# V's overlapping rows loaded once and copied on the chip, with a new issue order, in a one-core attention, mixture and MLP kernel

## The chip, the core and the metric

One core of a Trainium2 chip runs the whole program. The metric is the device time of one execution in microseconds, lower is better. The engines are TensorE (PE, with its weight loads PEld), VectorE (DVE), ScalarE (ACT), GpSimd (POOL) and SyncE (SP), which here only issues DMAs. Each engine works through its own instructions in the order in which the program issued them; semaphores tie the engines together.

## The reference

Three blocks in a row, all in float32, on B=2, H=8, S=768, D=64:

```
k_sum = k.reshape(B,H,24,32,D).max(3);  v_sum = v.reshape(B,H,24,32,D).mean(3)
scores_l = scale * q @ k.T,  kept where |i-j| < 16, else -1e9
scores_s = scale * q @ k_sum.T + log(32)
a = softmax(concat([scores_l, scores_s]));   x = a @ concat([v, v_sum])
# x as [B, S, 512] into 4 causal attention experts with top-2 gates,
# summed, then u = x + low-rank mix along S, out = u + relu(u @ w_ch1) @ w_ch2
```

The change touches the first block (the windowed attention) and one store at the very end.

## The kernel before, in words

**Stages.** The 16 heads form 8 pairs p = 0..7. A pair has 12 query blocks of 64 rows; a slot s covers four of these blocks for both heads, so a pair has 3 slots and the first block 24 slots. A query block of 64 rows sees a window of 96 keys (64 plus 15 or 16 on each side), so neighbouring windows overlap by 32 rows. After the first block come the projections and the causal attention of the experts (`v_proj`, `qk_proj`, `s_row`, `t_bank`, `pv`), then the merged MLP for batch 0 (`w1c`, `mlp1`, `mlp2`) and for batch 1 (`mlp1x`, `mlp2x`, `wide_sum`, `wide_store`).

**One pair of the first block.** `load_k`, `load_q` and `load_v` issue DMAs on SP. `load_v` (L377) brings V as the host has laid it out: for each head a tile of 96 partitions by 12 blocks by 65 numbers, block m holding rows 64m to 64m+95, so the 32 overlapping rows come twice from memory. There are three V buffers (`VWT`, one per p mod 3); the load of pair p+3 waits until the last `a_pv` of pair p has read the buffer. `kmax` (DVE) takes the maximum of K over 32 rows. `kcopy` (L404) spreads K into a window layout with the factor -1/8: per head columns 0 to 63, then columns 64 to 95, then the 24 block maxima; POOL does it for pairs 1 to 7, and for pair 0 it is split over POOL, ACT (`act.mul`, L412) and DVE. `fill_k` and `fill_q` write masks and identities into the other half of the partitions, once per buffer. `vsum` (L380) sums V over 32 rows on PE with a picking matrix, ACT and DVE add the four partial sums, and `vcast` (POOL) spreads them into the V tile.

**One slot.** `a_scores` (16 PE instructions in the trace, L431, then one DVE minimum, L434, and four ACT exponentials, L437), `a_trans` (4 transposes, L442, and one ACT copy, L444), `a_pv` (16 instructions, L454, then a reciprocal and a product on DVE) and `a_out` (2 transposes, L468, one ACT cast, L473, one DVE subtraction, L249).

**The order.** Every function is registered with `at(...)`; a function that yields is cut into parts. The table `TIMES` gives each part its place in one global order (0 to 1925), and `BANKS` gives each part its PSUM bank. That global order is what every engine's queue is made of; nothing is reordered later. The first PE work is `wake_up`: 24 products of a zeroed tile, to have PE busy from the start. `wake_zero` (L337) zeroes that tile on DVE.

**The end.** `wide_store` (L969) adds two parts of the last 256 rows' results and issues the stores on SP; the last row block is stored in two halves.

Of the kernel before, what the change touches and what calls it, by code (L numbers as in the profile page):

```python
# [22 lines left out]
NP = H // 2  # L23
QT = 64
# [7 lines left out]
KPAD = S + QT  # L32
# [3 lines left out]
def f(ap):  # L36
# [164 lines left out]
def tile_block_attention_moe_mixer(ctx: ExitStack, tc: tile.TileContext, qT, kP, vW, vB, wm, woT, wo,  # L201
# [134 lines left out]

    def wake_zero():  # L337
        dve.memset(wake, 0.0)

    def wake_up(n):  # L340
        for _ in range(n):
            pe.matmul(bank(7)[:, 0:128], wake, wake, start=True, stop=True)
# [34 lines left out]
    def load_v(p, h):  # L377
        nc.sync.dma_start(VWT[p % NBUF][0:WCOL, h], vW[p, :, h])
# [899 lines left out]
```

## Time and profile before

| | us |
|---|---|
| median of 3 runs | 426.53 |
| the three runs | 426.52, 426.53, 429.07 |
| the profiled execution, its own time | 428.55 |
| span of the profiled execution, first to last instruction | 426.7 |
| PE busy in it | 416.8 (98%) |
| DVE, ACT, POOL busy | 294.1, 242.7, 203.6 |
| moved by DMA | 35.01 MB |

The profiled execution took 428.55 us, of which 426.7 us lie between its first and its last instruction and 1.85 us around them. The granted TensorE clock was 1.000 over the span, which is the level of 2.4 GHz. A line of the trace names its engine, the kernel's line, what is written and read, the shape and the count; the time in brackets is what the engine stood idle before it, and for what. PE's ends are modelled, so the starts are the better guide to its pace.

### The profile page before, as it was taken

What the parts mean: (1) busy time and instruction counts of PE and PEld (TensorE: products, weight loads), DVE (VectorE), ACT (ScalarE), POOL (GpSimd) and SP (SyncE); (2) the same over time, 40 slices, a digit from 0 to 9 for tenths busy, and PEclk for the clock granted to TensorE, in tenths of its full rate; (3) what the DMA queues carried; (4) which work ended last, traced back from release to release, by engine and by line L of the source; (5) the groups of instructions that cost most, each with busy time, mean ns of one, the idle gap of its engine ahead of it and who ended that gap; (6) DMA issues with size and microseconds to landing.
All of it is one profiled execution on the core that took longest, in us unless ns stands there. A gap on an engine that the chain in (4) does not pass through costs nothing.

```text
span 426.7 us, 9493 instructions
## 1 busy us (share of the span) xinstructions
PE 416.8 (98%) x3568; PEld 384.0 (90%) x3568; DVE 294.1 (69%) x784; ACT 242.7 (57%) x615; POOL 203.6 (48%) x287
## 2 busy tenths in 40 slices
PE   7999999999999999999998999999999999999995
PEld 6898999999979898978897989989889999999995
DVE  6788745887658677877845885374577886755664
ACT  4589766566856696985555544452454355344341
POOL 6998765538886888643152642333543332000000
PEclk9999999999999999999999999999999999999999
DMA  8887670000212015312234452311103000100001
GB/s 218 222 218 210 200 168 2 3 0 20 68 51 78 0 51 174 100 50 95 89 109 153 147 167 86 124 69 51 49 27 123 2 2 1 51 2 0 26 26 49
DMA packets 14499, 35.01 MB, mean 82 GB/s; under 512 B 1907, under 2 KB 3187, under 8 KB 14454
## 3 DMA queue, kind: packets, MB, share of 16 engines
q1 hardware_dynamic: 14454, 34.41, 26.5%
q8 instruction: 28, 0.46, 0.4%
q14 instruction: 17, 0.14, 0.1%
HBM read 31.26 MB, written 3.15 MB: 81 GB/s over the span
## 4 chain that ended last, share of the span: by engine, by line
PE 44%; issue 4%; POOL 1%; DMA 1%; DVE 1%; DVEq 0%; POOLq 0%
PE ps L953 13%; PE ps L994 12%; PE ps L921 8%; PE ps L981 6%; PE ps L544 3%; PE ps L1003 2%; DMA x<-in_w_dram 1%; POOL x L276 1%; POOL m L276 1%; DVE a L971 0%; POOL m L910 0%; DVE a L988 0%; DVE a L963 0%; DVE a L962 0%; DVE a L965 0%
## 5 line engine op out<-in xcount | busy, mean ns | idle before, releaser
L246 POOL TENSOR_SCALAR a<-a 64x384 fp32r<-64x384 f32 x64 | 33.7, 527 | 12.8 <-ACT a L670 7.6
L981 PE MATMUL ps<-x,w1h 128*128 128x384 f32 x128 | 37.7, 341 | 1.6 <-DVE a L988 1.1
L921 PE MATMUL ps<-x,w1h 128*128 128x256 f32 x192 | 37.6, 282 | 0.0
L665 PE MATMUL ps<-x,m 128*128 128x384 f32 x192 | 36.4, 340 | 0.0
L665 PEld LDWEIGHTS ps<-x,m 128*128 128x128 f32 x192 | 33.2, 188 | 0.3 <-issue 0.2
L720 POOL TENSOR_SCALAR ex<-ex,rs,gate 128x512 f32<-128x512 f32 (+5 forms) x36 | 25.5, 716 | 12.1 <-ACT ex L707 5.6
L921 PEld LDWEIGHTS ps<-x,w1h 128*128 128x128 f32 x192 | 31.0, 189 | 0.2
L988 DVE SCALAR_TENSOR_TENSOR a<-ps,a 128x384 fp32r<-128x384 f32 x32 | 17.6, 552 | 18.9 <-ACT a L986 18.9
L986 ACT ACTIVATE a<-ps 128x384 fp32r<-128x384 f32 x32 | 15.6, 490 | 25.4 <-PE ps L981 23.1
L249 DVE TENSOR_TENSOR x<-x,x 128x384 fp32r<-128x384 f32 (+1 forms) x28 | 18.7, 677 | 14.5 <-ACT x L928 8.2
L696 PE MATMUL ps<-a 128*128 128x384 f32 (+4 forms) x128 | 27.8, 337 | 0.3 <-DVE lg L625 0.3
L921 PE MATMUL ps<-x,w1l 128*128 128x256 f32 x96 | 27.0, 282 | 0.0
L981 PEld LDWEIGHTS ps<-x,w1h 128*128 128x128 f32 x128 | 23.6, 188 | 3.6 <-DVE a L988 1.6
L704 DVE CUSTOM_DVE_ANT_0 ex<-ps,cc 128x384 f32<-128x384 f32 (+5 forms) x36 | 20.8, 598 | 8.6 <-PE ps L696 3.5
L994 PE MATMUL ps<-m,a 128*128 128x512 f32 x108 | 26.3, 392 | 0.0
L707 ACT ACTIVATE ex<-ex,nmx 128x256 f32<-128x256 f32 (+5 forms) x36 | 23.4, 651 | 3.7 <-DVE nmx L704 2.5
L267 DVE SCALAR_TENSOR_TENSOR x<-x 128x256 uint32<-128x256 uint32 (+3 forms) x38 | 23.6, 631 | 1.7 <-ACT x L265 1.7
L263 DVE TENSOR_SCALAR x<-x 128x256 uint32<-128x256 uint32 (+3 forms) x38 | 18.0, 479 | 9.2 <-DMA x<-in_w_dram 8.5
L994 PEld LDWEIGHTS ps<-m,a 128*128 128x128 f32 x108 | 20.1, 188 | 3.9
L737 ACT COPY pt<-ps 128x384 f32<-128x384 f32 (+1 forms) x40 | 19.9, 523 | 6.1 <-PE ps L729 4.3
L249 DVE TENSOR_TENSOR a<-a,a 128x384 fp32r<-128x384 f32 (+1 forms) x24 | 14.8, 622 | 10.4 <-ACT a L928 7.9
L265 ACT ACTIVATE x<-x 128x256 f32<-128x256 f32 (+3 forms) x38 | 20.7, 553 | 2.1 <-DMA x<-in_w_dram 2.0
(330 smaller groups left out, 1230.5 us busy)
## 6 DMA issues: line engine op xcount, KB each, us to landing
x<-in_w_dram SPq DMA_DIRECT2D x16, 512.0 KB, 3.6
x<-in_w_dram SPq DMA_DIRECT2D x20, 256.0 KB, 2.7
vb<-in_vW_dram SPq DMA_DIRECT2D x5, 585.0 KB, 5.7
a<-in_kP_dram SPq DMA_DIRECT2D x7, 416.0 KB, 6.2
out_dram<-a SPq DMA_DIRECT2D x11, 256.0 KB, 2.1
x<-in_wm_dram SPq DMA_DIRECT2D x4, 386.0 KB, 6.3
tb<-in_w_dram SPq DMA_DIRECT2D x6, 256.0 KB, 3.8
a<-in_w_dram SPq DMA_DIRECT2D x6, 256.0 KB, 2.9
```

What stands on the lines that cost most here:

```text
L246: pool.tensor_scalar(dst, src, 1.0, 0.0, op0=ALU.mult, op1=ALU.add)
L249: dve.tensor_tensor(dst, src, f(hi), op=ALU.subtract)
L267: dve.scalar_tensor_tensor(low, high, 3, low, op0=ALU.logical_shift_left, op1=ALU.bitwise_or)
L665: pe.matmul(acc, (WML if wl else WMH)[k][:, 128 * e:128 * e + 128], xt(b, k, xl)[:, c], start=n == 0, stop=n == 11)
L696: pe.matmul(flat[:, base + c0:base + c1], QS[u][:, 128 * i:128 * i + 128], kk[:, c0:c1], start=x == 0, stop=x == 1)
L704: dve.tensor_tensor_reduce(out=ex[:, 0:W], in0=flat[:, base:base + W], in1=cmask[:, S - W:S], scale=-1.0 / 8.0, scalar=3.0e38, op0=ALU.add ...
L707: act.activation(ex[:, 0:W], ex[:, 0:W], AF.Exp, bias=nmx, scale=-1.0, accum_out=sums)
L720: pool.tensor_scalar(ex, ex, rs[:, i % 2:i % 2 + 1], gate[b][:, i, e:e + 1], op0=ALU.mult, op1=ALU.mult)
L921: pe.matmul(acc[:, 256 * i:256 * i + 256], (W1L if wl else W1H)[q][:, c, 128 * (ff % 2):128 * (ff % 2) + 128], cp(1, c, xl)[:, o], start=m ...
L953: pe.matmul(acc[:, 256 * hf:256 * hf + 256], v[:, BLK[a]], w[wl], start=g < 2 and q == 0 and hf == 0 and i == 0, stop=q == 7 and i == 2, s ...
L981: pe.matmul(acc, (W1L if wl else W1H)[ff // 2][:, c, 128 * (ff % 2):128 * (ff % 2) + 128], cp(b, c, xl)[:, o], start=n == 0, stop=n == 5)
L994: pe.matmul(out_bank(b, 3 * j + t), a[:, 128 * t:128 * t + 128], w, start=False, stop=ff == 15 and x == 2, skip_group_check=True)
```

## The change

- **V.** For pair 0 the load stays. For pairs 1 to 7 `load_v` issues two DMAs: partitions 32 to 95 of both heads and all blocks, and partitions 0 to 31 of block 0 alone. The other 11 blocks' first 32 rows are copied on the chip by a new function `vdup`, one DVE copy for head 0 and one ACT copy for head 1, from partitions 64 to 95 of the block before.
- **K.** `kcopy` writes the 96 window columns with one instruction in place of two; K's padded length goes from 832 to 800 (`KPAD` to `KEND`).
- **Start.** `wake_zero` issues, behind the zeroing, a multiplication of one column on ACT, ahead of all other ACT work.
- **End.** The first half of the last row block's store is issued on ACT's queue in place of SP's.
- **Order.** `TIMES` and `BANKS` are replaced as a whole (761 functions with 1913 places in place of 774 with 1926).

```diff
-KPAD = S + QT
+KEND = S + WCOL - QT
 ...
     def wake_zero():
         dve.memset(wake, 0.0)
+        first = sm.tile([128, 1], F32, name="first", tag="first", bufs=1)
+        act.mul(first, wake[:, 0:1], 1.0)
 ...
     def load_v(p, h):
-        nc.sync.dma_start(VWT[p % NBUF][0:WCOL, h], vW[p, :, h])
+        vw = VWT[p % NBUF]
+        if p == 0:
+            nc.sync.dma_start(vw[0:WCOL, h], vW[p, :, h])
+        else:
+            nc.sync.dma_start(vw[32:WCOL], vW[p, 32:])
+            nc.sync.dma_start(vw[0:32, :, 0], vW[p, 0:32, :, 0])
+
+    def vdup(p):
+        vw = VWT[p % NBUF]
+        dve.tensor_copy(vw[0:32, 0, 1:], vw[64:WCOL, 0, 0:NQ - 1])
+        act.copy(vw[0:32, 1, 1:], vw[64:WCOL, 1, 0:NQ - 1])
 ...
         if o < WCOL:
-            src = KPT[p % 2][r, o:o + S].rearrange("p (m n) -> p m n", n=QT)[:, mm, 0:n]
+            t = KPT[p % 2][r, QT * mm.start:]
+            src = bass.AP(t.tensor, t.offset, [t.ap[0], [QT, mm.stop - mm.start], [1, n]])
 ...
-        nc.sync.dma_start(out[1, 128 * t:128 * t + 128, c], sb[:, c])
+        (nc.scalar if s == 2 and i and not c.start else nc.sync).dma_start(out[1, 128 * t:128 * t + 128, c], sb[:, c])
 ...
-                for o, n in ((0, QT), (QT, WCOL - QT), (WCOL, NB)):
+                for o, n in ((0, WCOL), (WCOL, NB)):
                     at(t + 0.001, kcopy, p, hh, mm, o, n)
+        if p:
+            at(A(PER * p) + Z["vs"] - 0.1, vdup, p)
```

Read off the old and the new `TIMES`, the order at the start is this (SP: DMAs; the number is the pair for loads, `vsum`, `vdup` and the slot for `a_...`):

| queue | before | after |
|---|---|---|
| SP | K0 (2), V0 (2), pick, K1, V1, Q0 (4), Q1 (2), eps, K2, Q2, eps, V2 | K0 (2), Q0 (3), pick, V1 (2), Q0, K1, V0, eps, V0, Q1, eps, Q1, K2, V2 (2), Q2 |
| PE | 18 wake-ups, vsum 0, 6 wake-ups, vsum 1, a_scores 0, 1, 2, a_trans 0, a_scores 3, 4, a_trans 1, 2, a_scores 5, a_pv 0, 1, 2, vsum 2 | 21 wake-ups, vsum 1, a_scores 0, 1, 2, vsum 0, a_trans 0, 1, 2 wake-ups, a_trans 2, 1 wake-up, a_scores 3, 4, 5, a_pv 0, 1, 2, vsum 2 |
| ACT | kcopy 0 in 4 pieces, fill_k, kcopy 0 in 4 pieces among two vsum copies, exponentials of slots 0, 1, 2, a_trans copies | the one-column product, kcopy 0 in 2 pieces, fill_k, vdup 1, kcopy 0 in 2 pieces, exponentials 0, 1, vsum 0, exponentials 2, vsum 1, a_trans copies, vdup 2, exponentials 3, 4 |
| DVE, ahead of a_scores 0 | masks, kmax 0, fill_k, vsum 0, kmax 1 | wake_zero, masks, fill_k, kmax 0, vdup 1, kmax 1 |

Later in the first block, `vsum` 6 moves from behind the first five `v_proj` parts to ahead of them. Between `a_pv` 11, which frees its V buffer, and `vsum` 6 PE then has eleven parts: `a_out` 8 to 11, `a_trans` 12 to 14, `a_scores` 15 and 16, `a_pv` 12 and 13.

## Rows read from the trace of the kernel before

**Rows 1.** The page's part 1: busy time, share and count by engine

```profile
PE 416.8 (98%) x3568; PEld 384.0 (90%) x3568; DVE 294.1 (69%) x784; ACT 242.7 (57%) x615; POOL 203.6 (48%) x287
```

**Rows 2.** Windows: length, PE, PEld, DVE, ACT, POOL busy, clock, DMA share, GB/s

```profile
2.00:12.50 10.50, 9.03 (x76) 8.36 (x76) 7.96 (x32) 5.30 (x11) 8.09 (x16) 1.00 1.01 259
...
22.50:51.00 28.50, 28.42 (x553) 26.06 (x552) 23.27 (x61) 24.75 (x74) 23.85 (x32) 1.00 0.79 217
```

**Rows 3.** Timeline of PE, first 25 us: start, length, line, count, idle before

```profile
2.32 6.44 PE L342 MATMUL ps<-vst 128*128 128x128 f32 x36 [2.32 <-DVE vst L338]
...
12.47 0.86 PE L385 MATMUL ps<-vb,cc 96*32 96x128 f32 x24 [0.35 <-DMA vb<-in_vW_dram]
13.27 0.43 PE L431 MATMUL ps<-pt,ex 128*64 128x120 f32 x4
...
14.14 0.39 PE L431 MATMUL ps<-pt,ex 128*64 128x120 f32 x4
...
20.89 1.10 PE L454 MATMUL ps<-vb,w1h 121*64 121x65 f32 x32
...
23.68 0.60 PE L442 MATMUL ps<-cc,tb 128*121 128x128 f32 x4
24.11 0.60 PE L442 MATMUL ps<-cc,ex 128*121 128x128 f32 x4
```

**Rows 4.** DMA issues of the page: count, KB each, median us to landing

```profile
vb<-in_vW_dram SPq DMA_DIRECT2D x5, 585.0 KB, 5.7
...
a<-in_kP_dram SPq DMA_DIRECT2D x1, 272.0 KB, 2.5
...
cc<-in_vB_dram SPq DMA_DIRECT2D x1, 27.0 KB, 4.5
```

**Rows 5.** Timeline of SP, first 14 us: start of the issue

```profile
2.58 0.43 SPq L353 DMA_DIRECT2D cc<-in_vB_dram  x1
...
13.23 0.29 SPq L347 DMA_DIRECT2D vb<-in_cst_dram  x1
```

**Rows 6.** Timeline of all engines, 1 to 15 us: what ACT, POOL, DVE do

```profile
1.27 0.20 DVE L327 TENSOR_SCALAR a<-a 64x96 f32<-64x96 f32 x1
...
2.10 0.17 DVE L338 MEMSET vst<- 128x128 f32 x1
...
3.79 1.28 ACT L412 ACT_TABLE_LOAD   x1 [3.79 <-DMA a<-in_kP_dram]
...
5.60 0.24 POOL L419 TENSOR_SCALAR pt<-a 64x64 f32<-64x64 f32 x1
...
6.85 0.40 DVE L365 COPY c<-a 64x480 f32<-64x480 f32 x1
6.86 0.50 POOL L419 TENSOR_SCALAR pt<-a 64x64 f32<-64x64 f32 x1
...
7.01 0.98 ACT L363 COPY c<-a 64x960 f32<-64x960 f32 x1
...
11.57 0.95 DVE L402 TENSOR_REDUCE ks<-a 128x24 f32<-128x768 f32 x1
...
13.07 0.82 POOL L419 TENSOR_SCALAR w1h<-a 64x768 f32<-64x768 f32 x1
...
14.45 0.51 POOL L419 TENSOR_SCALAR w1l<-a 64x384 f32<-64x384 f32 x1
```

**Rows 7.** Timeline of ACT: two sets of exponentials one behind the other

```profile
16.69 1.12 ACT L437 ACTIVATE ex<-ps,nmx 128x120 f32<-128x120 f32 x4
17.66 1.15 ACT L437 ACTIVATE pt<-ps,nmx 128x120 f32<-128x120 f32 x4
```

**Rows 8.** Waits of PE over the span: total us, times, longest

```profile
PE ps L981 <- DVE a L988: 1.1, 1, 1.1
```

**Rows 9.** Timeline of the end: the last sums on DVE, the last stores

```profile
422.14 1.35 DVE L971 TENSOR_TENSOR a<-ps,a 128x512 f32<-128x512 f32 x3
422.90 1.30 SPq L974 DMA_DIRECT2D out_dram<-a  x3
```

More of the change, by code (lines that the diff above doesn't have):

```diff
@@ L280, in tile_block_attention_moe_mixer @@
                                               ("pt0", S), ("tb", 512), ("w1h0", 2048), ("w1l0", 2048), ("w1l1", 2048),
-                                              ("w1h1", 2048), ("a1", 2 * KPAD), ("a0", 3 * S), ("woh", 1024), ("wol", 1024))}
+                                              ("w1h1", 2048), ("a1", 2 * KEND), ("a0", 3 * S), ("woh", 1024), ("wol", 1024))}
     KC, NK, NBUF = NQ * KCOL, 3, 3
-    KPT = [regs["a1"][:, o:o + KPAD] for o in (0, KPAD)]
+    KPT = [regs["a1"][:, o:o + KEND] for o in (0, KEND)]
     KWT = [[regs[n][:, 0:KC].rearrange("p (m n) -> p m n", m=NQ) for n in nn] for nn in (("pt1", "c32"), ("w1h0", "w1l0"))]
@@ L1040, in tile_block_attention_moe_mixer @@
         at(-29, wake_up, n)
-    KP, QP, VP, MP = (FIRST, KPAD), (256, S), (1, 2), (2, 4, NQ)
+    KP, QP, VP, MP = (FIRST, KEND), (256, S), (1, 2), (2, 4, NQ)
     at(-20, distances)
@@ L1211, in _layout @@
     pad = WIN - 1
-    kp = np.zeros((B * NP, 128, KPAD), k.dtype)
+    kp = np.zeros((B * NP, 128, KEND), k.dtype)
     kp[:, :, pad:pad + S] = k.transpose(0, 1, 3, 2).reshape(B * NP, 128, S)
```

284 rows, old and new, of tables (BANKS, TIMES) are left out of this document.

## The prediction

> **What bounds the kernel.** I read the totals by engine first, then the windows of the first block, PE's timeline of the start, the DMA issues with SP's timeline, and the end. The totals say that PE is the bound: 416.8 us busy of a span of 426.7 [rows 1]. The change removes no product, so it can only gain from PE's idle time: some 10 us, plus the wake-up products that stand at the start because nothing else is ready. In 22.5 to 51 us PE is busy 28.42 of 28.50 us; there the reader should look at the neighbours, ACT with 24.75, POOL with 23.85 and DVE with 23.27 us of 28.5 [rows 2]. They are hidden, but with little room.
>
> The room is at the two ends. At the start PE does wake-ups from 2.32 us; `vsum` 1 waits at 12.47 for V of pair 1, a_scores 0 follows at 13.27, and a_pv 0, from where PE has work without a break, starts at 20.89 [rows 3]. In 2 to 12.5 us the DMA engines are full, share 1.01 at 259 GB/s [rows 2]: the start is a question of which bytes come first. Then SP issues nothing more until 13.23, where it waits for DVE [rows 5]. At the end the last sums run from 422.14 and the three last stores are issued one behind the other from 422.90 for 1.30 us, 0.43 each [rows 9].
>
> **The start, step by step.** K0, V0 and the small pick tile, 1028 KB, had landed 4.5 us behind the pick's issue at 2.58, so at 7.1 [rows 4, 5]. In the new order V1 ends the first 1089 KB (K0 400, Q0 256, pick 27, V1 406). 61 KB more at 259 GB/s are 0.2 us: V1 lands at 7.3 in place of 12.47. `vdup` 1 on ACT moves 715 numbers per partition; between nothing and the 960 of L363 at 0.98 us [rows 6] I take 0.78 as an estimate by size. It ends at 8.1.
>
> PE's wake-ups: 36 instructions took 6.44 us [rows 3], 0.177 each. 42 now stand ahead of `vsum` 1. `wake_zero` takes the place where the masks began, 1.27 in place of 2.10 [rows 6], so PE starts near 1.5 and ends them at 8.9. So the wake-ups, not V1, release `vsum` 1: 8.9, and with its 0.80 (12.47 to 13.27) a_scores 0 comes at 9.7. What else does a_scores 0 need? Behind `vdup` 1 ACT has two kcopy pieces, by L363's pace 0.8 and 0.4: done at 9.3. In time. The table load of 1.28 us, which began only when K had landed at 3.79 [rows 6], now lies ahead of that landing; if it did not, 9.3 would be 10.6 and the start 0.9 later.
>
> Three a_scores at 0.87 (13.27 to 14.14) end at 12.3. `vsum` 0 needs V0, which now ends the first 2208 KB (1089, Q0 128, K1 400, V0 585, eps 6): 1180 KB behind the mark at 7.1, 4.7 us at full rate, so 11.8; but by the same sum V1 would have come at 11.0 before and came at 12.47, so up to 13.2. I take 12.5, and 13.3 behind `vsum`. Then three a_trans at 0.43 (23.68 to 24.11), three wake-up products of two instructions (1.1), three a_scores (2.6), and 0.1 to 0.2 for a change of kind here and there: a_pv 0 at 18.4 in place of 20.89, **-2.5 us**. Bounds: -2.9 with V0 at once, -2.1 with V0 at 13.2. POOL's merged K copies and K1 come inside this: K1 at some 10 us, then a DVE maximum of 0.95 [rows 6] ahead of the minimum of slot 0, 11.6 for a product that a_trans 0 uses at 13.3.
>
> **The first block.** Seven `vdup` add 7 x 0.78 = 5.5 us to ACT. On DVE 715 numbers cost more than the 0.40 of 480 [rows 6]; at most in proportion, 0.60: some 0.55, 3.9 us in all. In 22.5 to 51 us about four fall: 3.1 us on ACT against 3.75 idle, 2.2 us on DVE against 5.2 idle [rows 2]. ACT's busy time counts ends twice: two sets of exponentials of 1.12 and 1.15 us start 0.97 apart [rows 7], so its room is larger than it looks. I take them as hidden under PE; uncovered they cost up to 5.5. POOL saves: 768 and 384 columns cost 0.82 and 0.51 [rows 6], one of 1152 by the slope between them 1.15, 0.18 less; 14 of them give 2.5 us, hidden, so nothing. The memory traffic falls by 7 x 179 KB, some 5 us of a DMA that is not the bound behind 22.5 us (share 0.79): nothing. The small second DMA of 64 rows of 260 bytes: a tile with rows of 216 bytes came in among the full queues at the usual 4.5 us [rows 4], so nothing; the issue on SP, 0.43 more per pair, lies inside each load's time.
>
> The Trainium skill speaks against the DVE copy: "SBUF — State Buffer", section "SBUF: two separate sides", says that a DVE operation in a two-port mode and a GpSimd operation exclude each other for the whole instruction. The trace agrees: a POOL copy of 64x64 took 0.24 us alone and 0.50 beside the DVE copy of 0.40 [rows 6]. By that rule seven DVE copies push POOL back by 3.9 us at most, against the 2.5 saved.
>
> The one tight wait that I find is `vsum` 6. Between a_pv 11 and it PE has 4 a_out (half an a_trans each, 0.9), 3 a_trans (1.3), 2 a_scores (1.7) and 2 a_pv (32 instructions 1.10, so 1.0): 4.9 us. In that time V6 must be issued (0.43), land and be copied (0.78). For 390 KB the landing lies between 2.5 (272 KB) and 5.7 (585 KB) [rows 4]; by size 3.7. That makes 4.9, late by nothing, from -1.2 to +2.0. While ACT and DVE stand at this copy, exponentials and minima queue behind it, so I take **+0.3**. Pairs 3 and 4 have some 6.7 us by the same counting.
>
> **The middle and the end.** Behind the first block the products are the same in a new order. PE's longest wait there was 1.1 us, for DVE's L988 [rows 8]. Such waits may go or come: 0, bounds -1.5 and +2. At the end the middle store leaves SP's queue, so the last is issued one 0.43 earlier, less what its data is later: **-0.25** (0 to -0.43).
>
> **Sum.** -2.5 + 0.3 - 0.25 = -2.45. The profiled execution of 428.55 (span 426.7) would be 426.1. It lay 2.0 above the median, so against the median of 426.53 I forecast 424.1.
>
> **Rivals.** (A) The forecast: 422.9 to 425.6, chance 0.50. (B) Slower: ACT becomes the bound of the first block. A `vdup` stands in ACT's queue ahead of exponentials and can't start before V has landed. From the point where ACT's idle time, 3.75 us in 28.5, is used up, each 0.78 lies on the path: 424.1 + 5.5 = 429.6, and with V6 late by its full 2.0 instead of 0.3, 431.3. For it: ACT at 24.75 [rows 2]. Against: the pace of 0.97 [rows 7]. Chance 0.13. (C) The gain at the start doesn't come: the DMAs share their rate, V1, K1 and V0 all land near 12 us, and only the end is gained: 426.53 - 0.25 = 426.3. For it: V1 came 1.4 behind the sum. Against: the first 1028 KB did not wait for later ones. Chance 0.20. (D) More: the waits of the middle go too, 1.5 us: 422.6, with the start's best bound 422.2. Nothing in the profile speaks for it but their size. Chance 0.12. (E) POOL falls behind by the exclusion of the two engines: 3.9 - 2.5 = 1.4 us later, 425.5, if POOL is what PE waits for; nothing in the waits shows that it was. Chance 0.05.
>
> **The numbers.** A, C, D and E lie in 422.2 to 426.5; with the middle's bounds I give 421.6 to 428.3, which leaves out B and the tails. About 1%, 4.3 us, is what a measurement of this kernel tells from no change. Faster than 422.3: half of D and a little of A, 0.10. Slower than 430.8: half of B, 0.06. Within: 0.84.
>
> **What would show it.** `vsum` 1 before 9.5 us and a_pv 0 near 18.4 show the start right. ACT idle waiting for V's DMA ahead of L437, or PE waiting for ACT between 20 and 50 us, shows B. A wait of PE ahead of `vsum` 6 gives its price. If a_pv 0 comes 2.5 earlier and the span doesn't shrink by as much, the middle took it back.

## The result: slower by half a per cent

The changed kernel took 429.93 us (median of 7 runs, 428.98 to 430.62) against 427.38 us for the kernel before, measured again beside it (7 runs, 426.52 to 429.07). The ratio is 1.0053, 95% interval 1.0037 to 1.0069: some 2.3 us slower. The prediction was 424.1, with a range up to 428.3; both the sign and the range were wrong.

| | before | after |
|---|---|---|
| median | 427.38 | 429.93 |
| profiled execution, its own time | 428.55 | 428.98 |
| its span | 426.7 | 427.2 |
| moved by DMA, MB | 35.01 | 33.60 |

The two profiled executions differ by 0.4 us only. That of before lies near the upper end of its runs (a second one, below, took 426.72), that of after at the lower end of its own. These two alone would hide most of the difference.

Part 1 of the page of after, beside [rows 1]. PE's work is the same, DVE has 12.5 us more:

```profile
PE 417.0 (98%) x3568; PEld 384.9 (90%) x3568; DVE 306.6 (72%) x791; ACT 245.5 (57%) x619; POOL 204.4 (48%) x271
```

The two windows of [rows 2] in after. Up to 12.5 us the DMA engines are no longer full. From 22.5 to 51 ACT went from 24.75 to 27.16 of 28.50 us and DVE from 23.27 to 26.24, and PE lost 0.81 us of its busy time:

```profile
2.00:12.50 10.50, 9.77 (x94) 9.21 (x95) 8.75 (x33) 4.40 (x8) 5.73 (x11) 1.00 0.82 225
22.50:51.00 28.50, 27.61 (x530) 24.95 (x530) 26.24 (x62) 27.16 (x77) 25.44 (x28) 1.00 0.77 226
```

The start of after, beside [rows 3, 5, 6]: start, length, engine, line, count, idle before. Lines of PE, SP, ACT and DVE:

```profile
1.55 7.69 PE L342 MATMUL ps<-vst 128*128 128x128 f32 x42 [1.55 <-DVE vst L336]
...
6.67 0.43 SPq L380 DMA_DIRECT2D vb<-in_vW_dram  x1
...
7.63 0.79 ACT L388 COPY vb<-vb 32x715 f32<-32x715 f32 x1 [1.96 <-DMA vb<-in_vW_dram]
7.67 0.90 DVE L365 COPY w1h<-a 64x1440 f32<-64x1440 f32 x1
...
8.66 0.08 DVE L345 MEMSET w1l<- 32x24 f32 x1
8.77 0.27 SPq L347 DMA_DIRECT2D w1l<-in_cst_dram  x1
...
9.08 0.32 SPq L380 DMA_DIRECT2D vb<-in_vW_dram  x1
9.17 0.41 PE L395 MATMUL ps<-vb,cc 96*32 96x128 f32 x2
...
9.54 0.63 DVE L387 COPY vb<-vb 32x715 f32<-32x715 f32 x1
...
10.31 0.86 PE L395 MATMUL ps<-vb,cc 96*32 96x128 f32 x22 [0.73 <-DVE c L368]
11.10 0.43 PE L442 MATMUL ps<-pt,ex 128*64 128x120 f32 x4
...
14.34 0.87 PE L395 MATMUL ps<-vb,cc 96*32 96x128 f32 x24 [0.56 <-DMA vb<-in_vW_dram]
...
19.86 1.10 PE L465 MATMUL ps<-vb,w1h 121*64 121x65 f32 x32
```

V1 had landed by 7.63 and ACT copied its half at once. DVE copied the other half only at 9.54, behind a mask copy of 0.90 and small work, so `vsum` 1 stopped after two instructions and went on at 10.31. The wait is put down to L368, a short memset right behind the copy; what `vsum` needs is the copy. V0's second half was issued at 9.08, 2.4 us behind its first: between them SP stood at the eps load (L347), which needs a tile that DVE clears at 8.66 (L345). `vsum` 0 could start at 14.34.

The waits of PE of 0.5 us and more over the span in after (engine line waited for: total, times, longest), beside the one of [rows 8], and the same view of a second profile of the kernel before (the run e8 below):

```profile
PE ps L932 <- DVE a L999: 1.6, 1, 1.6
PE ps L342 <- DVE vst L336: 1.6, 1, 1.6
PE ps L395 <- DVE c L368: 0.7, 1, 0.7
PE ps L395 <- DMA vb<-in_vW_dram: 0.6, 1, 0.6
PE ps L395 <- DVE w1l L387: 0.5, 1, 0.5
PE ps L625 <- ACT pt L448: 0.5, 1, 0.5
```

```profile
PE ps L342 <- DVE vst L338: 2.3, 1, 2.3
PE ps L342 <- DVE vs L393: 1.2, 1, 1.2
PE ps L385 <- DMA vb<-in_vW_dram: 0.8, 1, 0.8
PE ps L981 <- DVE x L249: 0.5, 1, 0.5
```

The largest of after ends at 309.9 us; the DVE steps that lead to it begin near 305. The timeline of after around it:

```profile
304.04 0.69 DVE L908 TENSOR_TENSOR pt<-vb 128x512 f32<-128x512 f32 x1
...
305.00 1.51 POOL L274 TENSOR_TENSOR v<-x,v 128x512 fp32r<-128x512 f32 x1 [2.67 <-ACT v L272]
305.25 1.81 DVE L908 TENSOR_TENSOR pt<-vb 128x512 f32<-128x512 f32 x1
...
307.34 1.30 POOL L274 TENSOR_TENSOR v<-x,v 128x512 fp32r<-128x512 f32 x1 [0.84 <-ACT v L272]
307.42 1.50 DVE L911 TENSOR_TENSOR pt<-pt 128x256 f32<-128x256 f32 x1
308.85 1.01 DVE L999 SCALAR_TENSOR_TENSOR a<-ps,a 128x384 fp32r<-128x384 f32 x2
...
309.91 0.39 PE L932 MATMUL ps<-x,w1h 128*128 128x256 f32 x1 [1.63 <-DVE a L999]
```

Two additions of `tsum` 3 on DVE took 1.81 and 1.50 us where each ran into a POOL operation; the first of them, alone, took 0.69. Behind them stood L999, the last part of `mlp1`, which frees the PSUM bank that the first `mlp1x` products (L932) want.

The end, beside [rows 9]: the third store is on ACT's queue, but the last sum ends as late behind PE's last product as before.

```profile
422.67 1.35 DVE L982 TENSOR_TENSOR a<-ps,a 128x512 f32<-128x512 f32 x3
423.43 0.96 SPq L985 DMA_DIRECT2D out_dram<-a  x2
423.73 0.37 ACTq L985 DMA_DIRECT2D out_dram<-a  x1
```

### The profile page after: what moved, and what is told of

Read it like the earlier page. It is cut to its first block, busy times and chain, and to the rows that moved or that the text cites. A ratio compares the mean times of both kernels' runs of the same rounds, so it can differ in the third digit from the quotient of the medians.

```text
span 427.2 us, 9500 instructions
## 1 busy us (share of the span) xinstructions
PE 417.0 (98%) x3568; PEld 384.9 (90%) x3568; DVE 306.6 (72%) x791; ACT 245.5 (57%) x619; POOL 204.4 (48%) x271
## 2 busy tenths in 40 slices
DMA packets 14835, 33.60 MB, mean 79 GB/s; under 512 B 2467, under 2 KB 3747, under 8 KB 14790
## 4 chain that ended last, share of the span: by engine, by line
PE 86%; POOL 5%; DVE 3%; DMA 2%; SPq 1%; issue 1%; ACT 0%; DVEq 0%; POOLq 0%; ACTq 0%
PE ps L1005 14%; PE ps L964 13%; PE ps L932 8%; PE ps L676 8%; PE ps L992 7%; PE ps L555 5%; PE ps L707 5%; PE ps L740 4%; PE ps L758 4%; PE ps L625 4%; PE ps L1014 4%; PE ps L442 2%; PE ps L465 2%; PE ps L453 1%; DMA a<-in_kP_dram 1%; PE ps L479 1%
## 5 line engine op out<-in xcount | busy, mean ns | idle before, releaser
L932 PE MATMUL ps<-x,w1h 128*128 128x256 f32 x192 | 37.6, 282 | 1.6 <-DVE a L999 1.6
L932 PEld LDWEIGHTS ps<-x,w1h 128*128 128x128 f32 x192 | 30.9, 189 | 2.2 <-DVE a L999 2.1
L731 POOL TENSOR_SCALAR ex<-ex,rs,gate 128x512 f32<-128x512 f32 (+5 forms) x36 | 26.4, 739 | 9.1 <-DVE rs L726 3.3
L265 DVE SCALAR_TENSOR_TENSOR x<-x 128x256 uint32<-128x256 uint32 (+3 forms) x38 | 27.2, 724 | 3.3 <-ACT x L263 3.0
L707 PE MATMUL ps<-a 128*128 128x384 f32 (+4 forms) x128 | 28.9, 340 | 0.0
L999 DVE SCALAR_TENSOR_TENSOR a<-ps,a 128x384 fp32r<-128x384 f32 x32 | 17.4, 552 | 13.6 <-ACT a L997 13.5
L932 PE MATMUL ps<-x,w1l 128*128 128x256 f32 x96 | 27.0, 282 | 0.0
L247 DVE TENSOR_TENSOR x<-x,x 128x384 fp32r<-128x384 f32 (+1 forms) x28 | 17.0, 611 | 11.9 <-ACT x L939 9.4
L718 ACT ACTIVATE ex<-ex,nmx 128x384 f32<-128x384 f32 (+5 forms) x36 | 23.4, 652 | 3.6 <-DVE nmx L715 3.5
L992 PE MATMUL ps<-x,w1l 128*128 128x384 f32 x64 | 21.6, 337 | 0.0
```

The costliest lines, as they stand in the source:

```text
L265: dve.scalar_tensor_tensor(low, high, 3, low, op0=ALU.logical_shift_left, op1=ALU.bitwise_or)
L707: pe.matmul(flat[:, base + c0:base + c1], QS[u][:, 128 * i:128 * i + 128], kk[:, c0:c1], start=x == 0, stop=x == 1)
L718: act.activation(ex[:, 0:W], ex[:, 0:W], AF.Exp, bias=nmx, scale=-1.0, accum_out=sums)
L731: pool.tensor_scalar(ex, ex, rs[:, i % 2:i % 2 + 1], gate[b][:, i, e:e + 1], op0=ALU.mult, op1=ALU.mult)
L932: pe.matmul(acc[:, 256 * i:256 * i + 256], (W1L if wl else W1H)[q][:, c, 128 * (ff % 2):128 * (ff % 2) + 128], cp(1, c, xl)[:, o], start=m ...
L992: pe.matmul(acc, (W1L if wl else W1H)[ff // 2][:, c, 128 * (ff % 2):128 * (ff % 2) + 128], cp(b, c, xl)[:, o], start=n == 0, stop=n == 5)
```

## Which half of the order loses: e1 to e4

The first theory was the wait at 309.9 us, so that the loss lies in the order behind the first block; the rival was V's copies in the first block.

**e1_block_new**

```diff
 order and banks up to some 85 us: as changed
-behind it: as changed
+behind it: those of the kernel before
```

> The changed kernel's code (V split and copied, one K copy, early ScalarE product, store on ScalarE's queue) with the new order and banks up to the first expert's scores, some 85 us in, and from there the old order and banks. Theory 1 (the loss lies in the new order behind the first block, above all where VectorE and GpSimd meet at 303 to 310 us): 0.5 to 1 us faster than before or the same, 426.5 to 427.5. Theory 2 (the V copies load ScalarE and VectorE in the first block and cost the time): slower than before by 2 to 2.5 us.

432.37 us (6 runs), ratio 1.0123 (1.0089 to 1.0157). In its trace PE waited 1.9 us at 87 us for an ACT copy (L455), right where the two orders are joined; that wait is the edit's own. The profiled execution is the fastest of the six, 429.88 us at a granted clock of 0.999 over the span; the others take up to 435.08, the two longest at 0.990. So the trace does not show most of the 5.3 us, and the run shows only that the first block is no gain.

**e2_rest_new**

```diff
 order and banks up to some 85 us, V and K: those of the kernel before
-behind it: those of the kernel before
+behind it: as changed, with the store on ACT's queue
```

> The kernel before with its own code, order and banks up to some 85 us, and from there the new order and banks, with the store on ScalarE's queue. Theory 1 (new order behind the first block): slower than before by 2 to 2.5 us, the whole difference. Theory 2 (V copies in the first block): the same as before within 0.5 us.

428.20 us (12 runs), ratio 1.0010 (0.9991 to 1.0029). Read alone, the new rest costs nothing, and the first theory seems to fall. But its trace has the wait:

```profile
PE ps L921 <- DVE a L988: 1.7, 1, 1.7
```

So a null of 0.4 us held a wait of 1.7; the rest of the new order had to be gaining something as large. That is taken up with e9 and e10.

**e3_v_old_order**: the kernel before with V's two loads and `vdup` right ahead of each `vsum`, in the old order.

```diff
+vdup(p)
 vsum(p) part 0
```

> The kernel before with the V part alone: rows loaded once and copied by VectorE and ScalarE, the copy issued right ahead of each pair's vsum; order, banks and all else as before. Theory 1 (new order behind the first block costs): within 0.7 us of before. Theory 2 (V copies cost): slower by 2 us or more.

437.94 us (4 runs), ratio 1.0237 (1.0211 to 1.0263): the edit alone, in the old order, costs 10 us. Two of the waits of PE, those longest in total for `vsum`:

```profile
PE ps L396 <- DVE w1l L388: 3.7, 2, 1.9
...
PE ps L396 <- DVE woh L351: 1.9, 1, 1.9
```

`vsum` (L396) waits for the copies (L388 is DVE's) and for what is queued around them on DVE and ACT, 8.1 us over the span. Ahead of `vsum` 1 PE stood 1.87 us, to 14.31; the granted clock fell within that stop and stayed low behind it. Windows of the same run (columns as in [rows 2], the granted clock third from the end):

```profile
13.00:14.00 1.00, 0.00 (x0) 0.00 (x0) 0.91 (x3) 0.00 (x0) 0.88 (x3) 0.83 0.00 0
14.00:20.00 6.00, 5.69 (x65) 5.33 (x67) 1.66 (x9) 0.61 (x2) 4.66 (x8) 0.50 0.82 235
```

0.50 is the level of 1.2 GHz, for six microseconds of products; at 21 us the clock was 1.00 again. So a part of the 10 us is the clock.

**e4_no_v**: the changed kernel with V in full for all pairs, no `vdup`.

```diff
 ...
-        if p:
-            at(A(PER * p) + Z["vs"] - 0.1, vdup, p)
```

> The changed kernel with V loaded as before (all 96 rows for every pair, no copy), everything else and the order as changed. Theory 1 (new order behind the first block): as the changed kernel, 2 to 3 us slower than before, with vsum 1 some 1 us later at the start since 585 KB stand ahead of it. Theory 2 (V copies cost): back at the time of before.

430.36 us (12 runs), ratio 1.0044 (1.0026 to 1.0063), as slow as the changed kernel. Its PE waited 2.0 us for V's DMA, and its DMA engines were full (share 1.03) from 12 to 25 us. So V's copies are not the net loss in the new order. That they save DMA time there and cost as much on DVE and ACT fits the waits, but is not shown.

## Small parts and small repairs: e5 to e8

**e5_small_parts**: the kernel before in its own order with only the small parts.

```diff
-                for o, n in ((0, QT), (QT, WCOL - QT), (WCOL, NB)):
+                for o, n in ((0, WCOL), (WCOL, NB)):
 ...
+        act.mul(first, wake[:, 0:1], 1.0)
 ...
-        nc.sync.dma_start(out[1, 128 * t:128 * t + 128, c], sb[:, c])
+        (nc.scalar if s == 2 and i and not c.start else nc.sync).dma_start(out[1, 128 * t:128 * t + 128, c], sb[:, c])
```

> The kernel before, in its own order and with its own banks, with only the small parts of the change: K's buffer shorter, one copy for K's 96 columns, the early ScalarE product, the last store's right half on ScalarE's queue. V is loaded in full for all pairs. If the loss of the changed kernel comes from its new order in the first 85 us and from V's copies (theory 1), the small parts are worth nothing or a little: 0.2 us less at the end, 427.5 us, between 426.9 and 428.1. If the merged K copy or the early product makes one of DVE, ACT or POOL late for the first matrix products (theory 2), it is 1 us or more above the kernel before, 428.7 us or more, and the first a_scores start later than 13.7 us.

427.83 us (12 runs) against 427.51; ratio 1.0011 (0.9998 to 1.0023). The small parts, the store among them, are worth nothing.

**e6_copy_on_act**

```diff
-        dve.tensor_copy(vw[0:32, 0, 1:], vw[64:WCOL, 0, 0:NQ - 1])
+        act.copy(vw[0:32, 0, 1:], vw[64:WCOL, 0, 0:NQ - 1])
```

> The changed kernel with both halves of V's copy on ScalarE. In its trace the DVE half took 0.52 us alone but 2.15, 1.28 us and so on when a POOL operation ran, and TensorE then waited 0.55 to 0.8 us at 49 us for it. If that stretch beside POOL is part of the loss (theory 1), the copy costs ACT 0.79 us more for each of seven pairs, the wait at 49 us goes or falls below 0.3 us, and the time is 0.5 to 1 us below the changed kernel: 429.2 us, some 0.3% over the kernel before. If ScalarE is what bounds the first block (theory 2: it is busy 12.9 of the 13.0 us from 37 to 50), its 5.5 us more come out in the time: 431.5 us or more, with more waits of TensorE for ACT between 20 and 65 us.

431.38 us (6 runs), ratio 1.0096 (1.0072 to 1.0119): 1.8 us over the changed kernel. In the window from 22.5 to 51 us ACT was busy without a break, and PE 27.40:

```profile
22.50:51.00 28.50, 27.40 (x520) 24.88 (x517) 23.11 (x61) 28.15 (x83) 23.41 (x27) 1.00 0.72 194
```

ACT has no room there, though PE's busy time is only 0.21 us below that of the changed kernel in the same window. Its PE also waited 1.7 us for V0's DMA, to 14.59, and behind that stop the granted clock was 0.50 from 16 to 19 us. So not all of the 1.8 is ACT's, and the run does not show how much of it is.

**e7_two_waits**

```diff
-vsum(6), vsum(5): ahead of v_proj(0,4) and v_proj(0,0)
+vsum(6), vsum(5): behind them, vsum(5) on bank 2
-v_proj(0,5): behind a_scores(18)
+v_proj(0,5): behind the first part of qk_proj(0,0,0)
```

> The changed kernel with two places of its order mended: vsum 6 and vsum 5 start behind the first two parts of v_proj (vsum 5 on bank 2), and v_proj 5 of batch 0 starts behind the first part of qk_proj, so that neither waits: the first waited 0.8 us for the DVE copy of V at 49 us, the second 0.8 us at 68 us for the exponential that frees its bank. If these two waits are the loss of the first block (theory 1), the time is 1.2 to 1.6 us below the changed kernel: 428.5 us, some 0.2% over the kernel before. If ScalarE's load or another engine's sets the pace there (theory 2), the waits only move to the next instruction: 429.9 us, not over 0.4 us from the changed kernel.

434.80 us (6 runs), ratio 1.0179 (1.0148 to 1.0211): 5 us worse. Both waits went, but the first `qk_proj` now waited 1.5 us for the DVE sum that frees bank 2, and another product 1.1 for DVE's L472. Behind the first the granted clock was 0.50 from 58 to 61 us. The repair brought a worse wait of its own, so it tests neither theory.

**e8_before_again**: the kernel before, unchanged.

> The kernel before once more, for a second profile of it. In the first its TensorE waited 1.6 us near 191 us and 1.6 us near 229.8 us for weights; the changed kernel gained 2.5 us on it there and lost it again near 303 us. If these waits belong to the kernel, they stand again within 0.5 us, and the span is 425 to 427 us. If they belong to that one execution, one of them is missing and the span is 1 to 1.5 us shorter, which would mean that the gain in the middle is no gain over the median of before.

426.72 us, span 424.9. The 1.1 us wait for L988 of [rows 8] is not in it (its waits stand above). In the first profile that wait came of a weight load of 512 KB that took 6.1 us from issue to landing; here the same load took 4.3. So the wait belonged to one execution: what after gained on the first profile near 230 us is no gain over the kernel before.

## The wait near 305 us: e9 to e12

**e9_mlp_order**: the changed kernel, two steps moved. `one` is `mlp1` of batch 0.

```diff
 w2_split(15) part 2
+one(14,0) part 2          # DVE L999
 tsum(3) part 1            # DVE L908
-tsum(3) part 2            # DVE L910, L911
-one(14,0) part 2
 one(15,0) parts 0, 1, 2
+tsum(3) part 2
```

> The changed kernel with two DVE steps moved near 305 us: the last steps of mlp1 (line 999), which free the PSUM bank that the first wide mlp matmuls need, stand ahead of the additions of tsum 3 (lines 908 to 911) instead of behind them. In the traces of the changed kernel and of the three kernels with its order behind the first block TensorE stood 1.6 to 1.9 us there, since these additions took 1.81 and 1.50 us beside POOL instead of 0.69 and 0.41. Theory 1 (this wait is the largest single part of the loss): the wait goes, and the time falls by 1.2 to 1.8 us to 428.2 us, some 0.15% over the kernel before. Theory 2 (TensorE would have waited for the same DVE work a little later, or the loss lies in the first block): the time stays within 0.4 us of the changed kernel, 429.9 us.

427.50 us (11 runs) against 427.34; ratio 1.0005 (0.9994 to 1.0016). By the medians the wait is worth 2.1 us; in the two traces, 1.6. The timeline:

```profile
305.30 1.51 POOL L274 TENSOR_TENSOR v<-x,v 128x512 fp32r<-128x512 f32 x1 [2.71 <-ACT v L272]
...
305.64 0.56 DVE L999 SCALAR_TENSOR_TENSOR a<-ps,a 128x384 fp32r<-128x384 f32 x1
306.12 1.25 DVE L908 TENSOR_TENSOR pt<-vb 128x512 f32<-128x512 f32 x1
307.29 0.55 DVE L999 SCALAR_TENSOR_TENSOR a<-ps,a 128x384 fp32r<-128x384 f32 x1
...
307.76 1.43 DVE L910 TENSOR_TENSOR pt<-pt 128x256 f32<-128x256 f32 x1
...
308.36 0.28 PE L932 MATMUL ps<-x,w1h 128*128 128x256 f32 x1
```

The additions are still stretched beside POOL (1.25, 1.43), but nothing that PE needs stands behind them; L999, which reads PSUM, took its usual 0.56 beside POOL.

**e10_old_block_fix**: e2 with the same two steps moved.

> The order of before up to 85 us, the new order behind it (which came out at 0.5 us over the kernel before), with the same two DVE steps moved near 305 us. Theory 1: the new order gained some 1.9 us on the kernel before between 80 and 200 us and lost 1.7 us at 305 us; with that wait gone it is 1 to 1.5 us faster than the kernel before, 426.3 us. Theory 2: the gain between 80 and 200 us was only its late start made good, and the time is that of the kernel before, 427.4 us, within 0.5 us.

425.81 us (5 runs), ratio 0.9963 (0.9951 to 0.9975): 0.4% faster than the kernel before, and 0.9% faster than the changed one. With e2 at 1.0010 the wait is again worth 2.0 us, and what is left of the new rest is a gain of 1.6.

**e11_vproj_later**: only the `v_proj(0,5)` move of e7.

> The changed kernel with one thing moved in the first block: v_proj 5 of batch 0 behind the first part of qk_proj, and nothing else. It waited 0.55 us (0.8 us between two matmuls) at 68 us for the exponential that frees its bank. If that wait is a loss of its own (theory 1), the time is 0.5 to 0.8 us below the changed kernel, 429.2 us. If ScalarE, late by then, sets the pace (theory 2), the wait goes to the next matmuls that need one of its results, and the time stays at 429.9 us, or rises when a later wait is longer.

431.48 us (6 runs), ratio 1.0095 (1.0077 to 1.0114), 1.8 us worse than the changed kernel. The 0.5 us wait for ACT's exponentials went and one of 1.1 us for DVE's L472 came. That is the second theory's sign: the wait went to the next product. PE also waited 0.8 us for DVE's L247, which it had not before; that need not be the edit's. The 1.8 is not the first block's alone. The profiled execution is the longest of the six, 433.11 us. In it the wait for L999 ended at 312.55, and here the granted clock fell behind it, to 0.50 between 314 and 316:

```profile
314.00:315.00 1.00, 1.00 (x5) 0.93 (x5) 0.15 (x1) 0.00 (x0) 0.82 (x2) 0.50 0.00 0
```

The three executions with a granted clock of 0.997 or more over the span took 430.45 to 431.02 us, the three with 0.996 or less 431.93 to 433.11.

**e12_copy_on_pool**

```diff
-        dve.tensor_copy(vw[0:32, 0, 1:], vw[64:WCOL, 0, 0:NQ - 1])
+        pool.tensor_copy(vw[0:32, 0, 1:], vw[64:WCOL, 0, 0:NQ - 1])
```

> The changed kernel with the DVE half of V's copy on POOL. With both halves on ScalarE the time was 1.8 us over the changed kernel, so ScalarE has no room. On POOL the copy cannot be held up by POOL's own operation on the other engine, but stands in POOL's queue, behind operations of up to 1.8 us. If DVE is the tight engine of the first block (theory 1), the time falls by 0.5 us or more, to 429.4 us or less, and the wait at 49 us is shorter than 0.5 us. If it only matters when the copy is ready (theory 2), the copy on POOL ends later than that on DVE and the time is 1 us or more over the changed kernel: 431 us.

429.54 us (5 runs), ratio 1.0052 (1.0038 to 1.0065), the same as the changed kernel. PE waited 0.5 and 0.3 us for POOL's copies in place of DVE's. Neither theory is borne out: which of DVE and POOL copies doesn't matter. So DVE standing behind POOL is not by itself what makes the new first block slow.

## What is left of the early start: e13 and e14

**e13_new_start**: e10 with the changed order up to its first `a_trans`, with V's copy for pair 1 alone, and with the small parts of e5.

```diff
 ...
-        if p == 0:
+        if p != 1:
             nc.sync.dma_start(vw[0:WCOL, h], vW[p, :, h])
 ...
```

> The changed kernel's order up to its first a_trans (some 22 us), with V's copy for pair 1 alone; then the order of before to 85 us, and the new order with the two DVE steps moved near 305 us. All other pairs load V in full. The comparison is the run with the old first block and the same rest, which took 425.81 us. Theory 1 (the start's gain is real, and the new order of the first block gives it back): 1 to 1.5 us less, 424.6 us. Theory 2 (by 30 us both orders are held by the preparation of Q and K on POOL, busy 12 of 13 us from 12 to 25, and by the loads, so that no start helps): 425.8 us, within 0.5 us.

425.86 us (11 runs), ratio 0.9959 (0.9943 to 0.9976): the same as e10 within the noise. The old order of the block doesn't make the start's gain show in the time either.

**e14_new_start_no_v**: the same with V of pair 1 in full too.

> The same with V of pair 1 loaded in full too, so without any copy of V. If V's shorter load of pair 1 is what lets the start come early (theory 1), vsum 1 or a_pv 0 waits for its V, TensorE stands 1 us or more at 12 to 15 us, and the time is 0.7 us or more over the run with the copy. If the order of the loads alone does it (theory 2), both take the same within 0.4 us.

425.18 us (6 runs), ratio 0.9945 (0.9926 to 0.9965), the best of all runs; by the ratios it lies 0.6 us below e13 and 0.8 below e10, but the intervals overlap. PE's start in it:

```profile
9.29 0.86 PE L385 MATMUL ps<-vb,cc 96*32 96x128 f32 x24 [0.49 <-DMA vb<-in_vW_dram]
...
10.09 0.43 PE L432 MATMUL ps<-pt,ex 128*64 128x120 f32 x4
...
13.38 0.87 PE L385 MATMUL ps<-vb,cc 96*32 96x128 f32 x24 [0.61 <-DMA vb<-in_vW_dram]
```

V1 in full is in time but for 0.49 us, and a_scores 0 starts at 10.09, 1.0 us before that of the changed kernel, which waited for the copy. The shorter V is not what lets the start come early, as the second theory said, and the copy makes it later; the times lie further apart than that theory's 0.4 us, but not clearly.

What is left of the lead can be read at the first product of `v_proj`, behind the same stretch of the old order in e8, e10, e13 and e14 (the lines in this order):

```profile
51.48 3.15 PE L614 MATMUL ps<-m,x 128*128 128x260 f32 x24
51.55 3.15 PE L614 MATMUL ps<-m,x 128*128 128x260 f32 x24
51.00 3.15 PE L625 MATMUL ps<-m,x 128*128 128x260 f32 x24
50.36 3.15 PE L615 MATMUL ps<-m,x 128*128 128x260 f32 x24
```

Against e10, e13 is 0.55 us earlier there and e14 1.19.

To see where time goes between all the traces, each trace's products are added up in their order, each at the mean time that a product of its form takes from its start to the next one's start. Waits of over 0.1 us are left out of that mean, and wake-ups are not counted. The table says when each sum was reached, minus the same of e8, in us. These are single executions; the last row agrees within 0.2 with the differences of the spans.

```
work  time in e8   after    e9     e10    e13    e14
   2     13.7      -1.5   -1.5   +0.1   -1.5   -2.5
  10     22.6      -1.1   -1.2   +0.1   -0.8   -1.5
  20     33.0      -0.3   -0.4   +0.1   -0.5   -1.1
  35     48.3      -0.7   +0.1   +0.1   -0.5   -1.1
  40     53.3      +0.5   +0.9   +0.1   -0.5   -1.1
  55     67.8      +1.3   +1.7   +0.1   -0.5   -1.1
  80     92.8      +0.9   +1.3   +0.0   -0.2   -1.2
 200    214.6      -0.1   +0.3   -1.2   -1.4   -2.3
 290    302.9      +0.4   +0.7   -0.8   -1.0   -1.6
 300    312.9      +2.3   +0.7   -0.8   -1.0   -1.6
 400    412.1      +2.3   +0.7   -0.8   -1.0   -1.6
```

The new start is 1.5 us ahead at 14 us (2.5 without the copy). Half to four fifths of that is gone by 33 us: 0.76 us went to the three wake-up products that now stand behind `vsum` 0 (at 16.1 and 17.0 in after), some 0.8 to the waits for V0 and for an ACT exponential (0.56 and 0.21 in after), and e8 has 0.2 to 0.5 of small losses of its own in that stretch. In the old order of the block e13 and e14 keep what is left; at the end it is 0.2 and 0.8 us against e10. The ratios of the timed runs say the same, but their intervals don't tell either from nothing. In the new order after loses 2.0 us between 48 and 68 us, 1.2 and 0.8 around its two waits of 0.55, for DVE's copy ahead of `vsum` 5 and for ACT's exponential at 68.7. e9 loses 1.5 there without the first of these waits, so the waits alone are not the cause. Behind 313 us nothing changes any more.

## Why the prediction was wrong

By the timed runs the change comes apart like this: the new order behind 85 us, without its wait, -1.6 us (e10); the wait near 305 us, +2.1 (after less e9; e2 less e10 gives 2.0); the new first block, +1.8 (e9 less e10). These three add up to the measured +2.3 by the way they are taken; what checks them is that the wait costs the same with the old first block as with the new. The prediction had 0 and 0 for the first two, -2.2 for the block with its start, and -0.25 for the end.

1. **The start, -2.5.** The first steps held: PE's wake-ups from 1.55 (1.5), V1 landed by 7.63 (7.3), ACT's copy 0.79 (0.78), `vsum` 1 from 9.17 (8.9). Then a step was missing: the copy has a DVE half, and I placed only ACT's. It ran at 9.54, so a_scores 0 came at 11.10 in place of 9.7. The next was mis-sized: V0 came at 14.34, outside 11.8 to 13.2. I counted bytes at the full rate of [rows 2], but SP issued V0's second half only at 9.08, behind the eps load, which wanted a tile that DVE had to write first; [rows 5] had shown that load waiting for DVE. So a_pv 0 was 1.0 earlier, not 2.5. My bounds were added up wrongly besides: by the steps given, V0 at once makes -2.7 and V0 at 13.2 makes -1.8, not -2.9 and -2.1. And the step from there to the end, that an earlier a_pv 0 is worth its whole time because PE runs without a break from it, was wrong: of the 1.1 us of after against e8 there, 0.3 are left at 33 us. Even in the old order of the block the start is worth 0.2 us with the copy and 0.8 without it, neither clear of the noise.
2. **The first block, 0 and +0.3.** ACT's busy time in [rows 2] rose by 2.41 us where 3.1 was forecast, and DVE's by 2.97 where 2.2 was; I took this as hidden. The step that failed is that the block costs nothing but `vsum` 6: its new order costs 1.8 us. Nor is that simply the price of the copies: with V in full (e4) and with a copy on POOL (e12) the kernel is as slow. The new order itself had no term in my sum. `vsum` 6 did not wait, but `vsum` 5 behind it did, 0.55 where 0.3 was forecast. The nearness is luck: I had V6 land late, and what came late was DVE's copy. There the DVE copy took 2.15 us, where it takes 0.52 in another pair. In the timeline:

```profile
43.68 5.78 POOL L578 TENSOR_TENSOR m<-x,m 128x772 fp32r<-128x772 f32 x3
...
47.24 0.52 DVE L387 COPY vb<-vb 32x715 f32<-32x715 f32 x1
...
47.69 2.15 DVE L387 COPY w1l<-w1l 32x715 f32<-32x715 f32 x1
```

   So rival B was right that the block has little room left, ACT with 1.34 us idle of 28.5. That its 429.6 lies beside the measured 429.93 is luck: of what it named, PE waiting for ACT, the trace of after has only 0.7 us. By the table the loss of after lies between 48 and 68 us; how it divides between ACT, DVE and the new sequence of products stays open, since e6, e7 and e11 each made things worse.
3. **The middle, 0, with bounds of -1.5 and +2.** The new order goes on to the end of the program, so the change touches more than the first block and one store. Each bound was right in size: -1.6 and +2.1. Where the 1.6 are won stays open; by the table of traces e10 gains 1.2 between 93 and 215 us and gives 0.4 back. I left the middle at nothing because the trace of before can't show the waits of a new order. In fact 2.1 us hung on one place where DVE steps stood in the wrong order in front of one PSUM bank. That could be read from the change: the new `TIMES` has two parts of `tsum` 3 ahead of the last part of `one(14,0)`, the old one has them behind it.
4. **The exclusion of DVE and POOL.** I priced it as POOL pushed back by DVE's copies (rival E, 1.4 us). What cost PE came the other way round, at both places: DVE stood behind POOL. POOL was pushed back too, where the copy had begun first: its third 128x772 operation in the lines above began 0.02 us behind the first copy and took 2.20 us, the other two 1.83 and 1.84 (shortest, median and longest in ns):

```profile
L578 POOL TENSOR_TENSOR m<-x,m x3: 1832/1837/2197, 43.7 to 47.3; 128x772 fp32r<-128x772 f32 x3
```

   The page that I had cited, "SBUF — State Buffer" of the Trainium skill, section "SBUF: two separate sides", says that whichever starts first blocks the other, and that DVE operations with two SBUF inputs are concerned too, not copies alone. The trace agrees: the additions took 1.81 and 1.50 us behind a POOL operation, 0.69 and 0.43 without one. (The POOL copy of 0.24 us that I had called alone ran beside a small DVE operation.)
5. **The end, -0.25.** From PE's last product to the span's end it was 4.35 us before and is 4.27: -0.08, and e5 shows no gain.
6. **The base.** The median of three, 426.53, was low: later medians of before were 427.3 to 427.7. That is 0.8 us of the miss.

## What to carry to other kernels

A lead at the start is worth only what the stage behind it can use; here half of it or more was gone 20 us later, and in the new order all of it by 53 us. Where two changes come together, a null can be a gain and a loss: the new rest came out at +0.4 us, and with two DVE steps moved at -1.6. When work is moved to an engine, look up what stands in front of each piece in that engine's queue and whose operation it runs into, and put first whatever frees a bank or a buffer for the bound engine.

## What the runs showed of the hardware

- A DVE copy of 32x715 took 0.51 us with no POOL operation beside it (e9, at 49.47 us), 0.52 where it began ahead of a POOL operation of 128x772, and 2.15 where that operation had begun first; POOL's took 1.83 us, and 2.20 where the copy had begun first. A DVE addition of two SBUF tiles of 128x512 took 0.69 us alone and 1.81 behind POOL. DVE's operation on PSUM and SBUF (L999) took 0.54 to 0.56, also while POOL was at work, and ACT's copy of 32x715 0.78 to 0.79 in all seven pairs.
- A stop of PE of 1.5 to 1.9 us was followed by a granted clock of 0.50, the level of 1.2 GHz, for some 3 to 7 us in e3 (at 14 us), e6 (at 15), e7 (at 57) and e11 (at 313). Others of the same length were not: the clock stayed at 1.00 behind the stop of 1.63 us at 309.9 in after, those of 1.6 to 1.8 at the same place in e2, e4, e6, e7 and e12, and that of 1.86 at 89 us in e1. So neither the length of the stop nor its place in the program tells which it will be: e11 and after stop at the same products. By the table's reckoning this place cost 1.9 us in the trace of after and 3.5 in that of e11.
- One weight load of 512 KB took 6.1 us in one execution of the kernel before, 4.3 in another; by the table's reckoning that was worth 1.7 us of the first profile.
